# Tail tokens of two batches interleaved over all 128 partitions, with row patches on two queues and a new order of the closing steps

## The chip, the cores and the metric

The kernel runs on one core of one Trainium2 chip. The metric is the device time of one launch in microseconds, as the median of several runs; less is better. One execution has also been recorded by the hardware profiler, and all times of single instructions come from that execution. They count from the start of its span.

## The reference

The inputs are q, k and v (8 batches, 8 heads, 576 tokens, 64 per head) and the weights of a spectral layer: `w_r` and `w_i` (64 modes, 512 x 512 each) and `w_ch` (512 x 512). First comes causal attention with a window of 128 tokens and a linear bias per head. Its output x (8 x 576 x 512) goes through the spectral mix:

```
X = rfft(x, axis=1)                      # along the tokens
Y[:, :64] = X[:, :64] times (w_r + i w_i), one 512x512 matrix per mode
y = irfft(Y, n=576, axis=1)
u = x + y
out = u + max(u @ w_ch, 0)               # float32, 8 x 576 x 512
```

The output has 9.44 MB.

## The kernel before

**Stages.** Up to about 150 us the attention runs, unit by unit of a batch and four heads. From then to about 409 us the 64 modes are streamed: `acc` gathers the products of the transformed tokens with `w_r` and `w_i`, four modes at a time (a "quad"). The loads of the weights set the pace there. While they stream, TensorE also prepares what can be had early: the tokens times `w_ch` (`XW`) and, for all modes but the last ones, the rows of `Z` (mode rows of y) and of `ZW` (mode rows of y @ w_ch). From about 409 us the last quad is worked up, and then come the closing steps, in which the output is made and stored. Everything that the change touches takes effect in these closing steps.

**Tiles of the output.** 576 tokens are four tiles of 128 tokens and a tail of 64. A unit j of `units` is a pair of batches and one tile, so 128 x 2 x 512 outputs, 512 KB. Units 0 to 3 are batches 0 and 1, units 4 to 7 batches 2 and 3, 9 to 12 batches 4 and 5, and 13 to 16 batches 6 and 7. Units 8 and 17 hold the tails: unit 8 those of batches 0 to 3, unit 17 those of batches 4 to 7. In a tail unit before the change, batch b lies in the lower 64 partitions and batch b + 1 in the upper 64, and the second half of the free axis holds batches b + 2 and b + 3.

**Steps.** Two steps make a unit, and the order of all steps is a string written out by hand. `activate(j)`, written `a` and the unit's number, is the channel side: `begin` puts `XW` into the PSUM pair `mm`, `channels` adds the inverse transform of the upper modes' `ZW` (through `spread`, L626, with a quarter of the array per matmul), and ScalarE writes `r = relu(mm)`. For a unit in `POOLED`, GpSimd then adds the tokens x to r. `finish(j)`, written `f` and the number, is the token side: for a unit that is not in `POOLED`, `add_tokens` puts x into the PSUM pair `yy` through an identity matmul; `finish_tokens` adds the inverse transform of `Z`; VectorE writes `o = yy + r` (L780), and the store of `o` is issued. For a unit in `HALVES` the ScalarE and VectorE work and the store go in two pieces. `mm` and `yy` have two buffers each, `r` has six, `o` five.

**Queues.** SP issues the stores of full tiles (L782), each 512 KB, or 256 KB for half a unit. A tail unit is stored by two transfers of 64 partitions each (L790): one from SP for the lower half, one from GpSimd's queue for the upper half.

**Row patches.** The last quad's rows of `Z` and `ZW` [...] `patch` (L616) copies them by small transfers, one per batch. The steps wait for them: `a` of a pair of batches for its rows of `ZW`, `f` for its rows of `Z`. After the last matmul of the stream, SP patches `Z` of batches 0 and 1 and `ZW` of batch 0. GpSimd's queue patches, in this order, `Z` of batches 2, 3, 4, then `ZW` of 1, 2, 3, then `Z` of 5, 6, 7, then `ZW` of 4, 5, 6, 7. Its additions for `POOLED` units stand behind these on the same engine.

Of the kernel before, what the change touches and what calls it, by code (L numbers as in the profile page):

```python
# [11 lines left out]
BF16 = mybir.dt.bfloat16  # L12
# [8 lines left out]
P = 128  # L21
# [6 lines left out]
FULL = 4  # L28
# [371 lines left out]
def kernel(  # L400
# [10 lines left out]
    nc = tc.nc  # L411
# [11 lines left out]
    ident = const.tile([P, P], BF16, name="ident")  # L423
    F = const.tile([P, FULL + 2, 2 * NM], BF16, name="F")
    FT = const.tile([P, 2, S], BF16, name="FT")
# [33 lines left out]
    with ExitStack() as actx:  # L459
        at = _Attention(tc, actx, q, k, v, (ident, F, FT), x, XC, raw)  # L460
        n = len(at.units)
# [49 lines left out]
        for stage in range(min(lags), n + max(lags)):  # L511
            for name, arg, lag in STAGE:
                run(name, arg, stage - lag)
                if name in ("transpose", "exp") and side.get(stage):
                    for _ in range(1 + (name == "transpose")):
                        fn, h = side[stage].pop(0)
# [3 lines left out]
            if stage in AHEAD:  # L520
                if stage:
                    b, g = at.units[stage - 1]
# [5 lines left out]
    with ExitStack() as mctx:  # L528
# [14 lines left out]
        def late_end(acc, g, n):  # L543
# [19 lines left out]
            late_channels(zw, yT, yw, slice(0, DM))  # L563
            patch([(nc.gpsimd, b) for b in range(B)], yw, g, lambda b: ZW[:, b // 2, 1])

# [25 lines left out]
        ROWS = (LO, HI)  # L591

        def spectra(hf, bp, z, zw):
# [6 lines left out]
            for et in range(4):  # L600
                nc.tensor.matmul(zw, lhsT=lhsT[et], rhs=wch[:, et],
                                 start=(et == 0), stop=(et == 3))
            nc.scalar.copy(ZW[:, bp, hf], zw)  # L603
            for i in range(2):
# [7 lines left out]
        def patch(todo, rows, g, dst, lo=0, hi=8):  # L612

            for queue, b in todo:
                r = 64 * (b % 2) + 8 * (g % 8)
                queue.dma_start(out=dst(b)[r + lo : r + hi],  # L616
                                in_=rows.rearrange("(k v) e -> k v e", v=16)[lo:hi, b])

        def tokens(st, half):
            o = st * P + (64 * half if st < FULL else 0)  # L620
            return slice(o, o + 64)

        def spread(dst, half, b, hf, st, tok):

            row = ROWS[(b % 2) ^ (1 - hf)]
            nc.tensor.matmul(  # L626
                dst[ROWS[half]], lhsT=FT[row, b % 2, tokens(st, tok)], rhs=ZW[row, b // 2, hf],
                start=False, stop=True, skip_group_check=True,
            )

        units = []
# [5 lines left out]
        def token_tiles(j):  # L637
            b, st = units[j]
            return x[:, b : b + 2, st] if st < FULL else x[:, b + 1 : b + 4 : 2, FULL]
# [39 lines left out]
            if j + 1 < len(units):  # L679
                transposed(j + 1)  # L680

        POOLED, HALVES, FIRST = (3, 4, 8, 12, 16), (0, 1, 2, 7, 15), (0, 1)
        mms, yys, rs = {}, {}, {}

        def pair(tag, slot=0):
# [7 lines left out]
        def begin(j):  # L693

            slot = idle.pop(0)
            mm = pair("mm", slot)
            mms[j] = mm, slot
            b, st = units[j]
            for row in range(2):
                for n in range(2):  # L700
                    dst, c = (row, n) if st < FULL else (n, row)
                    nc.tensor.matmul(
                        mm[ROWS[c], dst], lhsT=ident[ROWS[row], ROWS[row]],
                        rhs=XW[ROWS[row], j, n], start=True, stop=False, skip_group_check=True,
                    )

        def channels(j):

            mm, b, st = mms[j][0], *units[j]
            for row in range(2):  # L710
                for n in range(2):
                    if st < FULL:
                        spread(mm[:, row], n, b + row, 1, st, n)
                    else:
                        spread(mm[:, n], row, b + row + 2 * n, 1, st, 0)

        def last_rows(ps, j, rows):

# [23 lines left out]
        def add_tokens(j):  # L742

            yy = yys[j][0]
            for n in range(2):
                nc.tensor.matmul(yy[:, n], lhsT=ident, rhs=token_tiles(j)[:, n],
                                 start=True, stop=False, skip_group_check=True)

        def finish_tokens(j):

            yy, b, st = yys[j][0], *units[j]
            for n in range(2):
                if st < FULL:
                    nc.tensor.matmul(  # L754
                        yy[:, n], lhsT=FT[:, n, st * P : (st + 1) * P], rhs=Z[:, b + n],
                        start=j in POOLED, stop=True, skip_group_check=True,
                    )
                    continue
                for half in range(2):
                    nc.tensor.matmul(  # L760
                        yy[ROWS[half], n], lhsT=FT[:, half, FULL * P :],
                        rhs=Z[:, b + half + 2 * n],
                        start=j in POOLED, stop=True, skip_group_check=True,
                    )

        def finish(j):

            b, st = units[j]
            if j == 0:
                last_rows(yys[0][0], 0, heads["yq"])  # L770
            else:
                if j not in yys:
                    take(j)
                if j not in POOLED:
                    add_tokens(j)
                finish_tokens(j)
            (yy, slot), r = yys.pop(j), rs.pop(j)
            o = heads["out"].tile([P, 2, DM], FP32, tag="o", bufs=5, name="o")
            for c in parts(j):
                nc.vector.tensor_tensor(out=o[:, c], in0=yy[:, c], in1=r[:, c], op=ALU.add)  # L780
                if st < FULL:
                    nc.sync.dma_start(  # L782
                        out=out[b + c.start : b + c.stop, st * P : (st + 1) * P].rearrange(
                            "b p e -> p b e"),
                        in_=o[:, c],
                    )
                    continue
                for half in range(2):
                    lo, hi = b + half + 2 * c.start, b + half + 2 * c.stop - 1
                    (nc.gpsimd if half else nc.sync).dma_start(  # L790
                        out=out[lo:hi:2, FULL * P :].rearrange("b p e -> p b e"),
                        in_=o[ROWS[half], c],
                    )
            free.append(slot)

        quads, side, recycle = [], [], list(again)
        ZW = Z = XW = FM = wch = w2 = None
        K1 = again[-1] + 1
        LAST = NM // 4 - 1
        for g in range(NM // 4):  # L800
# [5 lines left out]
            for i in range(8):  # L806
# [21 lines left out]
                for a in range(4):  # L828
                    nc.tensor.matmul(  # L829
                        into[32 * (i // 2) : 32 * (i // 2) + 32],  # L830
                        lhsT=window[a],
                        rhs=w[a],
                        start=(ri == 0 and a == 0), stop=(ri == (m > 0) and a == 3),
# [7 lines left out]
                if k == K1 - 1:  # L841
                    actx1.close()
                    w2 = mctx.enter_context(
                        tc.tile_pool(name="w2", bufs=NWB, side="right", reuse_waits="tile")
                    )
                    load_w(NWB, w2, False)
                    right = mctx.enter_context(
                        tc.tile_pool(name="late", bufs=1, side="right", reuse_waits="tile")
                    )
                    wch = right.tile([P, 4, DM], BF16, name="wch")  # L850
                    nc.gpsimd.dma_start(out=wch, in_=moe_w_ch.rearrange("(a p) e -> p a e", p=P))
                    ZW = right.tile([P, B // 2, 2, DM], BF16, name="ZW")
                    Z = right.tile([P, B, DM], BF16, name="Z")
                    XW = right.tile([P, len(units), 2, DM], BF16, name="XW")
                    FM = right.tile([P, 2, 2 * P], BF16, name="FM")
                    nc.gpsimd.memset(FM, 0.0)
                    for b in range(2):
                        nc.gpsimd.dma_start(
                            out=FM.rearrange("(k v) b s -> k v b s", v=16)[:, b, b],
                            in_=FT[64 * b + 56 : 64 * b + 64, b, : 2 * P],  # L860
                        )

                if quads:
                    if next(quads[0], True):
# [20 lines left out]
        yq, yT = heads[LAST]  # L885
# [10 lines left out]
                                    ident[96:, 96:])  # L896
            nc.vector.tensor_copy(yT[:, 2 * i : 2 * i + 2, 96:], tr[:, 2 * i : 2 * i + 2, 96:])
        patch([(nc.sync, 0), (nc.sync, 1)], yq, LAST, lambda b: Z[:, b])
        patch([(nc.gpsimd, b) for b in (2, 3, 4)], yq, LAST, lambda b: Z[:, b], 6)
        yw = F[:, : DM // (2 * NM)].rearrange("p a b -> p (a b)")  # L900
        for i, c in enumerate(sides):
            late_channels(zl[i], yT, yw, c)
# [8 lines left out]
        free.append(1)  # L911
        take(1)
        begin(1)
        channels(1)
        channel_rows = partial(patch, rows=yw, g=LAST, dst=lambda b: ZW[:, b // 2, 1])
        channel_rows([(nc.sync, 0)] + [(nc.gpsimd, b) for b in (1, 2, 3)])
        patch([(nc.gpsimd, b) for b in (5, 6, 7)], yq, LAST, lambda b: Z[:, b], 6)
        channel_rows([(nc.gpsimd, b) for b in (4, 5, 6, 7)])

        for step in ("a0 f0 a1 f1 a3 a2 f2 a7 f7 a4 f3 a5 f5 a16 a9 f4 f9 a12 a17 f16 f17 a8 "  # L920
                     "a13 f12 f13 a11 f11 a14 f8 a10 f14 a6 f10 f6 a15 f15").split():
            {"a": activate, "f": finish}[step[0]](int(step[1:]))


# [28 lines left out]
```

The softmax here doesn't subtract the row's maximum and nothing guards it: scores larger than these inputs give would overflow.

## Time and profile before

| what | us |
|---|---|
| median of 4 runs | 452.65 |
| lowest and highest | 451.78, 453.04 |
| the profiled execution, its own time | 452.27 |
| its span | 449.9 |
| TensorE busy | 355.3 |
| VectorE busy | 177.1 |
| ScalarE busy | 152.5 |
| GpSimd busy | 70.5 |

The span runs from the first to the last recorded instruction; the profiled execution's time has 2.4 us more around it. Engines: PE is TensorE's matmuls and PEld its weight loads, DVE is VectorE, ACT ScalarE, POOL GpSimd, SP SyncE; SPq is SP's queue. A busy share is an average over stages with different limits, so the closing steps have to be read in windows of their own. PEclk is the granted TensorE clock; it is 1.00 from 408 us until TensorE has done its work.

### The profile page before, as it was taken

How to read it: one execution, taken by the hardware profiler on the slowest of the kernel's cores; microseconds unless marked ns; L12 is line 12 of the kernel's file. 1: busy time of each engine (PE TensorE's matmuls, PEld its weight loads, DVE VectorE, ACT ScalarE, POOL GpSimd, SP SyncE). 2: the span in 40 equal slices, each digit the busy share in tenths (PEclk: the TensorE clock that was granted, in tenths of full speed). 3: DMA queues.
4: the chain of work that ended last, by engine and by line, in shares of the span. 5: the costliest groups of instructions: out<-in, count | busy, mean ns of one | idle time of the engine just before them, and what ended most of it. 6: DMA issues, size and time to landing. Idle time of an engine off the chain costs nothing.

```text
span 449.9 us, 8002 instructions
## 1 busy us (share of the span) xinstructions
PE 355.3 (79%) x3301; PEld 190.5 (42%) x3326; DVE 177.1 (39%) x322; ACT 152.5 (34%) x195; POOL 70.5 (16%) x125
## 2 busy tenths in 40 slices
PE   4788899999866485657467767999999999877992
PEld 3457777777653132212222233544444444323330
DVE  7879899998832011000010222121212202301783
ACT  6869899999810000000000010211122110101861
POOL 8600101012411100100000000000000000074960
PEclk8589999999999566675975798999999999999997
DMA  8999999999999999999999999999999999994697
GB/s 281 316 311 321 309 298 310 317 299 248 200 290 316 307 278 318 327 377 425 420 422 422 420 422 420 422 421 417 422 419 421 421 418 421 421 389 149 239 339 270
DMA packets 53524, 157.03 MB, mean 349 GB/s; under 512 B 5217, under 2 KB 24433, under 8 KB 41073
## 3 DMA queue, kind: packets, MB, share of 16 engines
q1 hardware_dynamic: 47440, 140.02, 80.9%
q0 software_dynamic: 6048, 16.50, 18.5%
q8 instruction: 26, 0.43, 0.4%
q14 instruction: 10, 0.07, 0.0%
HBM read 162.53 MB, written 9.44 MB: 382 GB/s over the span
## 4 chain that ended last, share of the span: by engine, by line
DMA 54%; PE 28%; DVE 10%; issue 2%; POOL 1%; SPq 1%; ACT 1%; DVEq 0%; POOLq 0%; ACTq 0%
DMA w<-in_moe_w_i_dram 17%; DMA w<-in_moe_w_r_dram 15%; DMA vr<-in_v_dram 12%; PE acc L829 10%; DMA vr<-in_moe_w_i_dram 8%; PE my L669 7%; DVE vb L233 3%; PE tr L648 2%; PE my L626 2%; DMA kr<-in_k_dram 2%; DVE x L347 1%; DVE att L305 1%; DVE k L238 1%; PE yy L754 1%; DVE vt L235 1%
## 5 line engine op out<-in xcount | busy, mean ns | idle before, releaser
L829 PE MATMUL acc<-w,XC 128*32 128x512 bf16 x456 | 129.7, 450 | 43.4 <-DMA w<-in_moe_w_r_dram 22.4
L829 PEld LDWEIGHTS <-XC 128*32 128x32 bf16 x508 | 59.3, 140 | 127.0 <-issue 92.7
L294 ACT ACTIVATE att<-sc 128x1024 bf16<-128x1024 f32 x64 | 64.0, 1031 | 8.3 <-PE sc L284 8.3
L603 ACT CAST ZW<-zw 128x512 bf16<-128x512 f32 x8 | 4.7, 586 | 159.8 <-DVE Z L605 126.5
L575 DVE TENSOR_SCALAR yq<-acc 128x512 bf16<-128x512 f32 x13 | 8.9, 688 | 105.2 <-PE acc L829 105.2
L678 ACT CAST XW<-my 128x512 bf16<-128x512 f32 x36 | 19.3, 589 | 77.6 <-PE my L626 77.6
L616 POOL DMA_DIRECT2D Z<-yq x20 | 10.3, 519 | 216.8 <-issue 210.3
L331 PE MATMUL av<-vb,att 128*128 128x132 bf16 (+1 forms) x576 | 38.4, 217 | 5.9 <-DVE x L347 4.2
L331 PEld LDWEIGHTS <-att 128*128 128x128 bf16 x704 | 36.5, 98 | 11.5 <-DVE x L347 8.5
L650 DVE COPY xT<-tr 128x1024 bf16<-128x1024 bf16 x18 | 12.4, 691 | 71.9 <-PE tr L648 71.9
L669 PE MATMUL my<-wch,xT 128*64 128x512 bf16 x288 | 34.5, 382 | 0.8 <-DVE xT L650 0.8
L256 ACT COPY qkT<-tp 128x1152 bf16<-128x1152 bf16 x30 | 33.5, 1115 | 2.4 <-PE tp L250 1.8
L284 PE MATMUL sc<-qkT 64*64 64x256 bf16 (+2 forms) x640 | 25.7, 269 | 5.2 <-ACT qkT L256 1.6
L347 DVE TENSOR_TENSOR x<-av,rec 128x640 bf16<-128x640 f32 x32 | 26.4, 824 | 1.1
L780 DVE TENSOR_TENSOR o<-yy,r 128x1024 f32<-128x1024 f32 (+1 forms) x23 | 21.8, 988 | 6.7 <-ACT r L737 3.4
L284 PEld LDWEIGHTS <-qkT 64*64 64x64 bf16 x640 | 14.8, 110 | 19.5 <-issue 16.2
L669 PEld LDWEIGHTS <-xT 128*64 128x64 bf16 x288 | 14.8, 109 | 19.0 <-issue 6.9
L233 DVE CAST vb<-vr 64x1024 bf16<-64x1024 f32 x32 | 22.2, 694 | 0.2
L737 ACT ACTIVATE r<-mm 128x1024 f32<-128x1024 f32 (+1 forms) x23 | 18.2, 838 | 7.5 <-PE mm L626 6.6
L305 DVE TENSOR_TENSOR att<-att,mask 128x1024 bf16<-128x1024 bf16 x32 | 20.6, 683 | 0.0
L605 DVE CAST Z<-z 64x512 bf16<-64x512 f32 x16 | 11.0, 689 | 22.9 <-PE z L598 22.7
L523 POOL COPY gate<-x 1x1 bf16<-1x1 bf16 x11 | 5.8, 524 | 86.1 <-DVE x L347 86.1
(124 smaller groups left out, 376.3 us busy)
## 6 DMA issues: line engine op xcount, KB each, us to landing
w<-in_moe_w_i_dram SPq DMA_DIRECT2D x52, 1024.0 KB, 17.0
w<-in_moe_w_r_dram SPq DMA_DIRECT2D x45, 1024.0 KB, 16.8
qr<-in_q_dram SPq DMA_DIRECT2D x16, 576.0 KB, 7.6
kr<-in_k_dram SPq DMA_DIRECT2D x16, 576.0 KB, 8.0
vr<-in_v_dram SPq DMA_DIRECT2D x64, 128.0 KB, 6.1
w<-in_moe_w_r_dram POOLq DMA_DIRECT2D x16, 512.0 KB, 17.4
out_dram<-o SPq DMA_DIRECT2D x11, 512.0 KB, 3.2
w<-in_moe_w_i_dram POOLq DMA_DIRECT2D x6, 512.0 KB, 7.5
```

Source lines behind the costliest of these rows:

```text
L233: nc.vector.tensor_copy(self.vb[u % 2][row, :, :, :, W * half : W * half + D], src[row, :2])
L256: (self.nc.vector.tensor_copy if u < 2 and w == "q" else self.nc.scalar.copy)(dst.rearrange("q h (p j) -> q h p j", j=TPP), tp.rearrange(" ...
L284: nc.tensor.matmul(sc[64 * half : 64 * half + 64, e, j * 256 + c0 : j * 256 + c0 + n], lhsT=qkT[row, 1, h, k0 + j : k0 + P : 2], rhs=qkT[r ...
L294: self.nc.scalar.activation(self.att[u % 2][:, kt * 8 * P : (kt + 1) * 8 * P], sc.rearrange("p e n -> p (e n)"), AF.Exp, scale=1.0 / math. ...
L305: nc.vector.tensor_tensor(out=rows, in0=rows, in1=self.table[:, heads], op=ALU.mult)
L331: nc.tensor.matmul(bank[:, qt * W : qt * W + rhs[j].shape[1]], lhsT=att[:, o : o + P], rhs=rhs[j], start=(n == 0 and j == 0), stop=(n == l ...
L347: nc.vector.tensor_tensor(out=self.x[:, b, :, cs].rearrange("p t (h d) -> p h t d", h=2), in0=tiles[:, :, :, :D], in1=rec.unsqueeze(-1).br ...
L669: nc.tensor.matmul(mm[ROWS[half]], lhsT=lhsT, rhs=wch[:, dt], start=(dt == 0), stop=False, skip_group_check=True,)
L678: nc.scalar.copy(XW[:, j, n], mms[n])
L737: nc.scalar.activation(r[:, c], mm[:, c], AF.Relu)
L780: nc.vector.tensor_tensor(out=o[:, c], in0=yy[:, c], in1=r[:, c], op=ALU.add)
L829: nc.tensor.matmul(into[32 * (i // 2) : 32 * (i // 2) + 32], lhsT=window[a], rhs=w[a], start=(ri == 0 and a == 0), stop=(ri == (m > 0) and ...
```

## The change

The change has four parts. They all lie in the work on units and patches.

1. Tail tokens alternate. In units 8 and 17, partition 2p holds token p of one batch and partition 2p + 1 token p of the other. Three tables made once, by a fill and six copies on GpSimd during the weight stream, do the interleaving inside the matmuls: `pairs` (a permutation, in the place of the identity), `FI` (the inverse transform of the tail with alternating columns, zero elsewhere) and `FC` (the same for the channel side). `begin` and `channels` of a tail unit are then two full matmuls each instead of four small ones, `finish_tokens` four full ones instead of four of 64 columns.
2. A tail unit is stored by two transfers of 128 partitions and 256 KB from SP, each one for two batches. GpSimd stores nothing any more.
3. `Z` of batch 2 is patched from SP. GpSimd's queue patches `Z` of 3, 4, 5, 6, then `ZW` of 1, 2, 3, then `Z` of 7, then `ZW` of 4 to 7.
4. `POOLED`, `HALVES` and the order of the steps are new. The tail units are no longer in `POOLED`, and they come last.

```diff
-        POOLED, HALVES, FIRST = (3, 4, 8, 12, 16), (0, 1, 2, 7, 15), (0, 1)
+        POOLED, HALVES, FIRST = (3, 6, 9, 12, 13, 14, 15), (0, 1, 2, 5, 8), (0, 1)
...
-            for row in range(2):
-                for n in range(2):
-                    dst, c = (row, n) if st < FULL else (n, row)
+            for n in range(2):
+                if units[j][1] == FULL:
+                    nc.tensor.matmul(mm[:, n], lhsT=pairs, rhs=XW[:, j, n],
+                                     start=True, stop=False, skip_group_check=True)
+                    continue
+                for row in range(2):
                     nc.tensor.matmul(
-                        mm[ROWS[c], dst], lhsT=ident[ROWS[row], ROWS[row]],
-                        rhs=XW[ROWS[row], j, n], start=True, stop=False, skip_group_check=True,
+                        mm[ROWS[row], n], lhsT=ident[ROWS[n], ROWS[n]],
+                        rhs=XW[ROWS[n], j, row], start=True, stop=False, skip_group_check=True,
                     )
...
-            for row in range(2):
-                for n in range(2):
-                    if st < FULL:
-                        spread(mm[:, row], n, b + row, 1, st, n)
-                    else:
-                        spread(mm[:, n], row, b + row + 2 * n, 1, st, 0)
+            for n in range(2):
+                if st == FULL:
+                    nc.tensor.matmul(mm[:, n], lhsT=FC, rhs=ZW[:, b // 2 + n, 1],
+                                     start=False, stop=True, skip_group_check=True)
+                    continue
+                for row in range(2):
+                    spread(mm[:, n], row, b + n, 1, st, row)
...
-                nc.tensor.matmul(yy[:, n], lhsT=ident, rhs=token_tiles(j)[:, n],
+                nc.tensor.matmul(yy[:, n], lhsT=ident if units[j][1] < FULL else pairs,
+                                 rhs=token_tiles(j)[:, n],
                                  start=True, stop=False, skip_group_check=True)
...
-                        yy[ROWS[half], n], lhsT=FT[:, half, FULL * P :],
-                        rhs=Z[:, b + half + 2 * n],
-                        start=j in POOLED, stop=True, skip_group_check=True,
+                        yy[:, n], lhsT=FI[:, half], rhs=Z[:, b + half + 2 * n],
+                        start=False, stop=True, skip_group_check=True,
...
-                for half in range(2):
-                    lo, hi = b + half + 2 * c.start, b + half + 2 * c.stop - 1
-                    (nc.gpsimd if half else nc.sync).dma_start(
-                        out=out[lo:hi:2, FULL * P :].rearrange("b p e -> p b e"),
-                        in_=o[ROWS[half], c],
+                for n in range(c.start, c.stop):
+                    nc.sync.dma_start(
+                        out=out[b + 2 * n : b + 2 * n + 2, FULL * P :].rearrange("h p e -> p h e"),
+                        in_=o[:, n],
                     )
...
+                    FI = right.tile([P, 2, P], BF16, name="FI")
+                    FC = right.tile([P, P], BF16, name="FC")
+                    pairs = right.tile([P, P], BF16, name="pairs")
+                    nc.gpsimd.memset(FI, 0.0)
+                    for i, rows in enumerate((slice(0, 64), slice(64, P))):
+                        nc.gpsimd.tensor_copy(FI[:, i, i::2], FT[:, i, FULL * P :])
+                        nc.gpsimd.tensor_copy(pairs[:, i::2], ident[:, rows])
+                        nc.gpsimd.tensor_copy(FC[rows], FI[rows, i])
...
-        patch([(nc.gpsimd, b) for b in (2, 3, 4)], yq, LAST, lambda b: Z[:, b], 6)
+        patch([(nc.sync, 2)] + [(nc.gpsimd, b) for b in (3, 4, 5, 6)], yq, LAST, lambda b: Z[:, b], 6)
...
-        patch([(nc.gpsimd, b) for b in (5, 6, 7)], yq, LAST, lambda b: Z[:, b], 6)
+        patch([(nc.gpsimd, 7)], yq, LAST, lambda b: Z[:, b], 6)
         channel_rows([(nc.gpsimd, b) for b in (4, 5, 6, 7)])

-        for step in ("a0 f0 a1 f1 a3 a2 f2 a7 f7 a4 f3 a5 f5 a16 a9 f4 f9 a12 a17 f16 f17 a8 "
-                     "a13 f12 f13 a11 f11 a14 f8 a10 f14 a6 f10 f6 a15 f15").split():
+        for step in ("a0 f0 a1 f1 a3 a2 f2 a5 f5 a6 a10 f3 f10 a15 a4 f6 f4 a13 a16 f15 f16 "
+                     "a12 f13 a11 a9 f11 f12 a7 a14 f7 a8 f9 a17 f14 f17 f8").split():
```

Up to the first closing step both programs issue the same work on TensorE, in the same order.

More of the change, by code (lines that the diff above doesn't have):

```diff
@@ L697, in begin @@
             mms[j] = mm, slot
-            b, st = units[j]
-            for row in range(2):
-                for n in range(2):
-                    dst, c = (row, n) if st < FULL else (n, row)
+            for n in range(2):
[4 more added lines that the diff above has]
+                for row in range(2):
                     nc.tensor.matmul(
-                        mm[ROWS[c], dst], lhsT=ident[ROWS[row], ROWS[row]],
-                        rhs=XW[ROWS[row], j, n], start=True, stop=False, skip_group_check=True,
+                        mm[ROWS[row], n], lhsT=ident[ROWS[n], ROWS[n]],
+                        rhs=XW[ROWS[n], j, row], start=True, stop=False, skip_group_check=True,
                     )
@@ L796 @@
         quads, side, recycle = [], [], list(again)
-        ZW = Z = XW = FM = wch = w2 = None
+        ZW = Z = XW = FM = FI = FC = pairs = wch = w2 = None
         K1 = again[-1] + 1
```

## The prediction

> **What bounds the kernel now.** The first view is the page's slices: up to some 409 us the weight stream holds the DMA near 420 GB/s, and nothing of the change reaches into that stage except a few table copies. So I read the closing steps, 418 us to the end, in windows of one microsecond (columns: length, then busy us and count of PE, PEld, DVE, ACT, POOL, then PEclk, the DMA's busy share, GB/s).
>
> ```profile
> 425.00:426.00 1.00, 1.00 (x13) 0.39 (x11) 1.00 (x2) 0.47 (x1) 0.94 (x1) 1.00 0.09 35
> 433.00:434.00 1.00, 0.98 (x10) 0.36 (x11) 1.00 (x2) 0.55 (x2) 1.00 (x1) 1.00 0.86 178
> 434.00:435.00 1.00, 1.00 (x11) 0.24 (x9) 0.92 (x2) 0.72 (x1) 0.85 (x1) 1.00 1.02 240
> 440.00:441.00 1.00, 1.00 (x8) 0.31 (x4) 0.81 (x2) 0.74 (x2) 0.00 (x0) 1.00 0.97 258
> 443.00:444.00 1.00, 0.00 (x0) 0.00 (x0) 0.00 (x0) 0.00 (x0) 0.00 (x0) 1.00 1.03 389
> ```
>
> Two things are full here: PE has no free time until 441.2, and the stores then run on for six more microseconds with every engine idle. So at the end the bound is the store queue, fed by a PE that is itself full. The queue has lost time in two ways: it starved at 425 (35 GB/s), and twice it was busy at a low rate (178 and 240 GB/s at 433 to 435, 258 at 440). The low rates are the tail units' stores, of 64 partitions each. The two store lines say so; the answer for L782 comes first, that for L790 second:
>
> ```profile
> L782 SPq DMA_DIRECT2D out_dram<-o x21: 332/372/1213, 417.7 to 444.1; - x21
> DMA to landing us min/median/max: 2.2/4.3/6.3
> ...
> L790 SPq DMA_DIRECT2D out_dram<-o x2: 725/792/860, 431.8 to 437.1; - x2
> DMA to landing us min/median/max: 4.7/5.0/6.5
> ```
>
> In the trace's packet records, a 2 KB packet of a full store takes 84 ns (16 engines, so 512 KB in 256/16 x 84 = 1.345 us); from 433.0 to 434.5, when the lower half of unit 17 is stored, the medians of half-microseconds are 149, 162 and 193 ns. Last, PE's own steps and their waits:
>
> ```profile
> 424.14 0.41 PE L702 MATMUL mm<-XW,ident 64*64 64x512 bf16 x4
> 424.70 0.80 PE L626 MATMUL mm<-ZW,FT 64*64 64x512 bf16 x4
> ...
> 427.72 0.60 PE L702 MATMUL mm<-XW,ident 64*64 64x512 bf16 x4
> 428.15 0.60 PE L626 MATMUL mm<-ZW,FT 64*64 64x512 bf16 x4
> 428.68 0.60 PE L754 MATMUL yy<-Z,FT 128*128 128x512 bf16 x2
> 429.12 0.59 PE L746 MATMUL yy<-x,ident 128*128 128x512 bf16 x2
> 429.65 0.62 PE L760 MATMUL yy<-Z,FT 128*64 128x512 bf16 x4
> 430.20 0.65 PE L702 MATMUL mm<-XW,ident 64*64 64x512 bf16 x6
> ...
> 435.11 0.62 PE L760 MATMUL yy<-Z,FT 128*64 128x512 bf16 x4
> 435.66 0.41 PE L702 MATMUL mm<-XW,ident 64*64 64x512 bf16 x4
> 435.90 0.39 PE L626 MATMUL mm<-ZW,FT 64*64 64x512 bf16 x4
> 436.22 0.61 PE L746 MATMUL yy<-x,ident 128*128 128x512 bf16 x2
> ...
> 437.19 0.41 PE L702 MATMUL mm<-XW,ident 64*64 64x512 bf16 x4
> ```
>
> From start to start: an ordinary `a` takes 435.66 to 436.22, 0.56 us; an `f` with its tokens 436.22 to 437.19, 0.97; a pooled `f` 428.68 to 429.12, 0.44, and 0.53 where a change of shape follows (f3, 422.08 to 422.61 in the same view). The tail steps are a17 0.96 (427.72 to 428.68), f17 1.08 (429.12 to 430.20), f8 0.55 (435.11 to 435.66). The first two lines are a16: 0.5 us lost waiting for the `ZW` rows of batches 6 and 7.
>
> **The change part by part: PE.** Three more ordinary units are pooled (seven, was four): -3 x 0.43 = -1.3 us. Full matmuls follow each other at 0.216 us (two tokens matmuls 0.43). A tail `a` becomes four of them, 0.87 and a change of shape of 0.1: 0.97. A tail `f` becomes six, 1.40: f17 +0.3, f8 +0.85, since it also loses its pooling.
>
> What a tail `a` cost before is where a rule speaks against the change. The trace has 0.96. The Trainium skill (TensorE: Matmul & The Clock Gate, Part 3: Packing small matmuls) says that small matmuls on different tiles of the array run together, so eight quarter matmuls should take the 0.56 of an ordinary `a`, and full ones would add 0.4 for each tail. The row decides: a17 ran only two at a time (its four L702 rows start at 427.72 and 427.93), as both of `n` use the same two quarters. So 0 for a17, 0.1 for a8 (with a13 it took 1.42, less 0.56). By the row the PE sum is -1.3 + 0.3 + 0.85 + 0.1 = 0; by the rule +0.7. I take 0.
>
> **Patches.** SP gets one more small issue (0.6 us) between its `Z` patches and its `ZW` of batch 0. It ends at about 415.7, and `ZW` waits for its rows until 415.63 anyway; the first store is at 417.70. On POOL:
>
> ```profile
> 416.37 1.64 POOL L616 DMA_DIRECT2D ZW<-F  x3 [0.95 <-ACT F L570]
> 418.00 1.55 POOL L616 DMA_DIRECT2D Z<-yq  x3
> 419.54 2.16 POOL L616 DMA_DIRECT2D ZW<-F  x4
> ```
>
> The fourth `Z` patch of the first group fits into the 0.95 us that POOL waits for F, and two of the three at 418.00 are gone, so `ZW` of 4 to 7 is issued at 418.5 to 420.7, 1.0 us earlier, and POOL's additions begin at 420.7 instead of 421.7.
>
> Against this, a10 needs `ZW` of 4 and 5 and moves from near the end to the eleventh place. The steps a5, f5, a6 before it cost what a7, f7, a4 cost in their place, and a4 ended at 422.08; so a10 begins then and wants its rows at 422.32. The landings of that stretch have a straggler: one DMA engine was held 1.2 us by a 16 KB instruction fetch at 420.3. The patches issued at 418.53 and 419.04 had 15 of 16 parts by 420.85 and 421.86, and the last at 423.04 and 423.68. `ZW` of 5 will be issued at 419.07, so I put it at 423.7. The bounds: 422.0 (no straggler, no stall) and 425.0 (the longest landing of L616, 5.9 us). So PE stands 1.3 us (0 to 2.6) before a10; f3, f10 and everything after stand behind it, and the next store with them. The 0.5 us before a16 goes, as a15 comes three us after its rows.
>
> **Sum on PE.** a10 ends at 424.0. Then come 7 pooled `f` x 0.53, 5 `f` x 0.97, 9 `a` x 0.56, 2 tail `a` x 0.97 and 2 tail `f` x 1.40: 18.4 us. With 0.15 where a9 waits for ScalarE to free its buffer, PE ends at 442.5 (441.2 before).
>
> **Stores.** o3 leaves DVE (1.22 us) at 425.8; its packets start 0.86 after (as of the store issued at 425.14). So the starved gap is 425.0 to 426.7, 0.7 longer. From there 14 units at 1.345 are 18.8 us: 445.5, with small gaps (0.5) 446.0, and 0.4 to the landing. From the other side: f8's halves leave DVE at 443.25 and 443.85, and the last 256 KB needs at least the 2.2 of L782, with the SP issue as slow as L790's (0.79) 2.9: 446.1 to 446.8. Both say 446.5. Before, the last landing was at 448.8 and the span ended 1.1 after. The new span is 447.6; I add 0.4 for the DMA engine that is behind, as landings of one store lay up to 1.9 apart at the end: **448.0, against 449.9, so -1.9 us**. In the profiled execution that is 452.27 to 450.4; its own time lies 0.38 under the median, so the median goes from 452.65 to about **450.7**.
>
> That rests on the new tail stores running at 84 ns a packet. The trace has no such store. Its nearest row by shape, L790, says 149 to 193 ns; the Trainium skill (SBUF — State Buffer, Door 1: The DMA port swizzle) says that 64 partitions reach half of the 16 ports and all 128 reach all. By the row four tail stores at the end cost 4 x 1.3 us, by the rule 4 x 0.67: 2.6 us apart. I take the rule, for the full stores next to it have 128 partitions and 84 ns.
>
> **At nothing.** The tables: seven GpSimd instructions behind 183.7, where POOL has nothing until 394; if POOL were not idle they would delay the patches of the last-but-one quad. POOL's two more additions (2.13 each): it loses two store issues (0.65 each) and starts 1.0 earlier; a14's r is ready at about 439.5 and VectorE turns to f14 at 439.9, a margin of 0.3 to 0.4. VectorE keeps 1.22 beside them: o<-yy,r takes 1.224 at 423.9 with POOL adding and 1.225 at 437.3 without. SP's two extra-long tail issues are in the 2.9 above.
>
> **The rivals.** (1) a10 does not wait: the straggler comes elsewhere and the rows land by 422.3. Then everything is 1.3 earlier: span 446.5, median 449.3. For it: 15 of 16 parts were there by 421.9. Against: the fetch follows from PE's place in its program, which is the same up to here. Chance 0.13. (2) The gain goes under: the stall is 2.6, or the store queue starves again wherever PE feeds it two `a` in a row. Span 449.0 to 449.9, median 452.2; 0.15. For it: PE, not the queue, would then set the end, and it ends later. (3) Slower: the tail stores are slow as such and now stand last, with nothing behind to overlap. From 442.6, four of them at x us each, then 1.5 to the end: 450.8 (slower by over 0.9) is reached from x = 1.7, or 210 ns a packet. At 291 ns, the longest in L790's time, x = 2.3, span 453.4, median 456. For it: L790 is also slow to issue (0.79 against 0.37). 0.12. That the change doesn't do what it says is no separate case: its stores could only fail as in (3).
>
> **Numbers.** The forecast has 0.60. A measurement of this kernel tells about 0.2%, 0.9 us, from no change. Faster is forecast and (1), 0.73; same is (2), 0.15; slower (3), 0.12. The range takes in (1) and (2): 449.0 to 452.6.
>
> **What would show it.** Right: no slow window with GB/s under 300 at a full share after 427; the last store lands within 3 us of its issue; a10's L626 starts near 423.7; PE ends near 442.5 and the stores near 446.5. Wrong: tail packets over 150 ns; a wait of a10 over 3 us; DMA gaps after 428.

## The result and the profile after

The changed kernel has a median of 452.33 us over 35 runs, the kernel before 453.33 over 56 runs beside them. The ratio is **0.9972, interval 0.9959 to 0.9985**: faster by 0.28%, which is 1.3 us of 453 (0.7 to 1.9). The forecast was 1.95 us. (The prediction started from 452.65, the median of the first 4 runs of the kernel before.) The profiled execution took 450.89 us with a span of 448.8, against 452.27 and 449.9: the span is 1.1 us shorter where 1.9 were forecast.

The span moves with the weight stream, which the change doesn't touch: in the profiles shown below the stream ends anywhere from 411.8 to 415.0 us. So the kernels are compared here by their **closing span**, from the start of the matmul `zl<-wch,ident`, the first after the stream, to the end of the span. It was 37.01 us before (412.88 to 449.90) and is 35.94 after (412.82 to 448.76). Each is read from one profile; the timed ratio stands beside it.

The windows of the changed kernel, in the columns used above:

```profile
425.00:426.00 1.00, 1.00 (x18) 0.38 (x16) 1.00 (x2) 0.06 (x2) 0.36 (x1) 1.00 0.08 29
426.00:427.00 1.00, 0.66 (x9) 0.21 (x3) 0.98 (x2) 1.00 (x2) 0.00 (x0) 1.00 0.26 96
434.00:435.00 1.00, 1.00 (x17) 0.38 (x16) 1.00 (x2) 0.32 (x2) 1.00 (x2) 1.00 1.03 377
440.00:441.00 1.00, 0.94 (x6) 0.36 (x4) 0.91 (x2) 0.00 (x0) 0.00 (x0) 1.00 1.04 391
445.00:446.00 1.00, 0.00 (x0) 0.00 (x0) 0.00 (x0) 0.00 (x0) 0.00 (x0) 0.50 1.01 381
446.00:447.00 1.00, 0.00 (x0) 0.00 (x0) 0.00 (x0) 0.00 (x0) 0.00 (x0) 0.50 0.18 68
447.00:448.00 1.00, 0.00 (x0) 0.00 (x0) 0.00 (x0) 0.00 (x0) 0.00 (x0) 0.50 0.03 10
```

The slow windows are gone: 377 and 391 GB/s where there were 240 and 258. The starved gap is longer: 425 to 426.7 instead of 425 to 426. The last two lines are the surprise. At 446 to 448 the DMA is nearly idle (0.18, then 0.03) and yet the kernel waits. The landing records say for what. A store counts as done when its sixteen parts have landed, and the last stores of the changed kernel landed like this:

```
last packets of the store   15 of 16 parts   the 16th
issued at 442.27            445.26           446.53
issued at 443.35            445.95           447.15
issued at 444.02            446.62           447.79
```

One part in sixteen is late in every store that lands after 437 us, by 1.8 us at first (438.40 against 440.18) and by 1.2 in the end, and in none of those that land from 428 to 436 (there all sixteen lie within 0.3). At 437.12 the trace has one packet of 16 KB on the instruction queue, which took 948 ns. It is the one packet of this line of the DMA view from 436 to 439 us (packets, MB, share of the 16 engines):

```profile
q8 instruction: 1, 0.02, 2.0%
```

TensorE's program is fetched in such pieces: the recorded weight loads and matmuls between two of them are 254 on average in this trace, 184 to 349 in single cases. The one before came at 420.1 and took 1532 ns.

The other place is a10, in the timeline of TensorE:

```profile
421.92 0.39 PE L704 MATMUL mm<-XW,ident 64*64 64x512 bf16 x4
422.91 0.40 PE L626 MATMUL mm<-ZW,FT 64*64 64x512 bf16 x2 [0.61 <-DMA ZW<-F]
423.55 0.40 PE L626 MATMUL mm<-ZW,FT 64*64 64x512 bf16 x2 [0.23 <-DMA ZW<-F]
423.88 0.61 PE L758 MATMUL yy<-Z,FT 128*128 128x512 bf16 x2
```

a10's first matmuls run at 421.92 and its last at 423.55, where without a wait they would run at 422.14. The first pair waits for the `ZW` rows of batch 4 (15 parts landed by 421.09, the last at 422.87), the second for those of batch 5 (15 by 421.97, the last at 423.50): 1.4 us in all for a sixteenth part, and f3 stands behind it.

### The profile page after: what moved, and what is told of

It is laid out like the page before. It is cut to its first block, busy times and chain, and to the rows that moved or that the text cites. A ratio compares the mean times of both kernels' runs of the same rounds, so it can differ in the third digit from the quotient of the medians.

```text
span 448.8 us, 7986 instructions
## 1 busy us (share of the span) xinstructions
PE 356.0 (79%) x3290; PEld 190.4 (42%) x3314; DVE 177.1 (39%) x322; ACT 152.2 (34%) x195; POOL 74.5 (17%) x131
## 4 chain that ended last, share of the span: by engine, by line
DMA 54%; PE 30%; DVE 9%; issue 2%; ACT 1%; POOL 1%; SPq 1%; POOLq 1%; DVEq 0%; ACTq 0%
DMA w<-in_moe_w_r_dram 29%; PE acc L831 11%; DMA vr<-in_v_dram 9%; PE my L669 7%; DMA vr<-in_moe_w_r_dram 7%; DMA w<-in_moe_w_i_dram 6%; DVE vb L233 3%; PE tr L648 2%; PE my L626 2%; DMA qr<-in_q_dram 2%; PE av L331 1%; DMA kr<-in_k_dram 1%; PE yy L758 1%; DMA ZW<-F 1%; DVE k L238 1%
## 5 line engine op out<-in xcount | busy, mean ns | idle before, releaser
L831 PE MATMUL acc<-w,XC 128*32 128x512 bf16 x456 | 132.0, 455 | 41.3 <-DMA w<-in_moe_w_r_dram 22.8
L331 PEld LDWEIGHTS <-att 128*128 128x128 bf16 x704 | 36.5, 98 | 11.1 <-DVE x L347 8.1
L669 PEld LDWEIGHTS <-xT 128*64 128x64 bf16 x288 | 14.8, 109 | 18.9 <-issue 6.9
```

Source lines behind the costliest of these rows:

```text
L331: nc.tensor.matmul(bank[:, qt * W : qt * W + rhs[j].shape[1]], lhsT=att[:, o : o + P], rhs=rhs[j], start=(n == 0 and j == 0), stop=(n == l ...
L669: nc.tensor.matmul(mm[ROWS[half]], lhsT=lhsT, rhs=wch[:, dt], start=(dt == 0), stop=False, skip_group_check=True,)
L831: nc.tensor.matmul(into[32 * (i // 2) : 32 * (i // 2) + 32], lhsT=window[a], rhs=w[a], start=(ri == 0 and a == 0), stop=(ri == (m > 0) and ...
```

## The experiments

Theory A: full-width tail stores bring the gain; the order gives part of it back at a10; and the instruction fetch at 437 puts one DMA engine behind, which the full store queue keeps behind up to the end. Its rivals differ by run: that the late part has nothing to do with the fetch, that the order or the patches bring the gain, that the width of a store matters little. "PE ends" is the end of the last matmul. All ratios are to the kernel before on the same chip.

| run | ratio (95% interval) | closing span, us | PE ends, us of it | last store: 15 parts, 16th |
|---|---|---|---|---|
| before | 1 | 37.01 | 28.3 | spread over 1.9 |
| changed | 0.9972 (0.9959 to 0.9985) | 35.94 | 28.9 | 33.8, 35.0 |
| x1_fetch_late | 0.9925 (0.9898 to 0.9952) | 33.48 | 27.5 | 32.5, 32.5 |
| x2_fetch_early | 0.9931 (0.9902 to 0.9961) | 34.41 | 27.6 | 32.4, 33.4 |
| x3_tails_only | 0.9971 (0.9944 to 0.9998) | 35.86 | 29.5 | 34.0, 34.9 |
| x4_old_patches | 0.9991 (0.9965 to 1.0017) | 36.27 | 29.2 | 34.1, 35.2 |
| x5_order | 0.9928 (0.9902 to 0.9954) | 34.24 | 27.7 | 32.3, 33.3 |
| x6_half_stores | 1.0056 (1.0030 to 1.0081) | 39.50 | 29.0 | spread over 0.9 |
| x7_tails_only_fetch_late | 0.9935 (0.9910 to 0.9960) | 34.96 | 29.5 | 34.0, 34.0 |
| x8_before_fetch_late | 0.9991 (0.9970 to 1.0013) | 37.08 | 28.3 | spread over 1.9 |
| x9_order_fetch_late | 0.9918 (0.9886 to 0.9951) | 33.51 | 27.7 | 32.5, 32.5 |

**x1_fetch_late.** Only the number of warm-up matmuls at the very start changes, 400 us away from the place in question.

```diff
-        for _ in range(24):
+        for _ in range(2):
             nc.tensor.matmul(wt, lhsT=ident, rhs=ident, start=True, stop=True)
```

> The changed kernel with 2 instead of 24 warm-up matmuls at the very start, so that TensorE's program is 44 instructions shorter ahead of the closing steps and nothing in the closing steps changes. In the traces a 16 KB instruction fetch comes with every 256 TensorE instructions, at 420.1 and 437.1 us in the changed kernel, and the last parts of every store after 437 land 1.2 us after the other fifteen. Theory A (the fetch at 437 puts one DMA engine behind, the full store queue keeps it behind, and that is the 0.8 us that the prediction lacks): the last fetch falls behind the end of the program, all sixteen parts of the last store land within 0.3 us, and the fetch of 420 comes at about 422.5, behind the patches that a10 waits for, so that its wait of 1.3 us shrinks to under 0.5. The closing span (from the zl<-wch,ident matmul near 412.8 to the end; 37.0 us before, 35.9 after) becomes 33.7 to 34.6. Theory B (the late engine is late for its own sake, or from the tail stores' shape): one part still lands 1 us behind and the closing span stays at 35.9 +- 0.3, or loses 0.3 from a10 alone.

The fetches came at 9.1 us of the closing span and at 35.5, after the end (7.3 and 24.3 in the changed kernel). The sixteen parts of the last store landed within 0.3 us. a10 had its rows: TensorE's timeline, and then the last windows:

```profile
420.87 0.39 PE L704 MATMUL mm<-XW,ident 64*64 64x512 bf16 x4
421.09 0.47 PE L626 MATMUL mm<-ZW,FT 64*64 64x512 bf16 x4
421.49 0.60 PE L758 MATMUL yy<-Z,FT 128*128 128x512 bf16 x2
```

```profile
443.00:444.00 1.00, 0.00 (x0) 0.00 (x0) 0.00 (x0) 0.00 (x0) 0.00 (x0) 1.00 0.73 275
444.00:445.00 1.00, 0.00 (x0) 0.00 (x0) 0.00 (x0) 0.00 (x0) 0.00 (x0) 0.82 0.00 0
```

The second of these lines is not what the changed kernel showed: the DMA goes from 0.73 to nothing, with no thin trail. The closing span fell by 2.46 us, a little more than expected. The time is 0.75% under the kernel before: the same closing steps, instruction for instruction, give 1.3 us or about 3.4, by where the fetches fall. Theory A holds, and the rival falls. The fetch at 9.1 us still makes a part late (by 0.9 us at 423.33), but no step waits for it.

**x2_fetch_early.** The program is made longer instead of shorter, so that only the first fetch leaves the critical place.

```diff
-        for _ in range(24):
+        for _ in range(36):
...
-            for _ in range(3):
+            for _ in range(5):
                 wt = ps.tile([P, DM], FP32, tag="my", bufs=2, name="my")
```

> The changed kernel with 12 more warm-up matmuls at the start and 22 more during the last weights of the stream: TensorE's program is 68 instructions longer ahead of the closing steps, which are themselves unchanged. The fetches should come near 416.5, before the first store, and near 432. Theory A: a10's rows are no longer late by one part, its wait of 1.3 us falls to 0.3 or less and the starved gap at 425 to 426.5 shrinks by the same; but the second fetch again puts one engine about 1.2 us behind up to the end. Closing span 34.6 to 35.2 (35.9 in the changed kernel). Theory B (the fetch has nothing to do with either): a10 waits 1.3 us as before, closing span 35.9 +- 0.3. If the additional matmuls hold up the stream, its end (409.0) comes later, which the closing span leaves out.

The fetches came at 2.6 and 18.9 us. a10 waited for nothing, PE ended as in x1, and the last part was late again, by 1.0 us, with the thin trail at the end:

```profile
443.00:444.00 1.00, 0.00 (x0) 0.00 (x0) 0.00 (x0) 0.00 (x0) 0.00 (x0) 1.00 1.01 383
444.00:445.00 1.00, 0.00 (x0) 0.00 (x0) 0.00 (x0) 0.00 (x0) 0.00 (x0) 0.59 0.09 33
445.00:446.00 1.00, 0.00 (x0) 0.00 (x0) 0.00 (x0) 0.00 (x0) 0.00 (x0) 0.50 0.01 4
```

So the two costs come apart: 1.53 us from the rows of a10 (35.94 to 34.41), 0.93 from the late part at the end (34.41 to 33.48). The split rests on one profile of each run; the timed ratios of x1 and x2 don't tell these two apart. It is also the control for x1: a longer start gives most of the same gain, so the gain isn't from a shorter start.

**x3_tails_only.** The kernel before with the tables, the tail matmuls and the tail stores of the change, in the old order:

```diff
-        POOLED, HALVES, FIRST = (3, 4, 8, 12, 16), (0, 1, 2, 7, 15), (0, 1)
+        POOLED, HALVES, FIRST = (3, 4, 12, 16), (0, 1, 2, 7, 15), (0, 1)
...
-                for half in range(2):
-                    lo, hi = b + half + 2 * c.start, b + half + 2 * c.stop - 1
-                    (nc.gpsimd if half else nc.sync).dma_start(
-                        out=out[lo:hi:2, FULL * P :].rearrange("b p e -> p b e"),
-                        in_=o[ROWS[half], c],
+                for n in range(c.start, c.stop):
+                    nc.sync.dma_start(
+                        out=out[b + 2 * n : b + 2 * n + 2, FULL * P :].rearrange("h p e -> p h e"),
+                        in_=o[:, n],
                     )
```

> The kernel before with the interleaved tail units and their stores of 128 partitions alone: old order, old patches, old sets of pooled and halved units, except that unit 8 can't be pooled any more. Theory A (the full-width stores bring the gain, and the new order and patches give some back): no slow window at 433 to 435 and 440 to 442, tail packets at 84 to 88 ns instead of 149 to 193; PE ends 1.25 later, at about 442.4; closing span 35.0 to 36.0 against 37.0 before. Rival (the order and the patches bring the gain): closing span 36.6 to 38, as PE has 1.25 us more to do and sets the end.

It has the whole gain by itself: closing span 35.86, ratio 0.9971 against 0.9972. PE ends 1.2 later than before, as expected, and the stores make more than that good. The windows of its two tail units:

```profile
433.00:434.00 1.00, 0.95 (x10) 0.31 (x4) 1.00 (x2) 0.48 (x1) 0.00 (x0) 1.00 1.03 385
440.00:441.00 1.00, 1.00 (x11) 0.26 (x10) 1.00 (x2) 0.07 (x1) 0.00 (x0) 1.00 1.01 379
```

(From 434 to 435 it has 303 GB/s at a share of 0.84: there the queue ran short, and its packets still took 86 to 88 ns.) So with the fetches about where they were, the new order, the sets and the patches add nothing measurable to the tail units. x3 changes three things at once in those units: the width of their stores, the queue of half of them (GpSimd's before, SP's now) and their matmuls.

**x4_old_patches.** The changed kernel with the old patches:

```diff
-        patch([(nc.sync, 2)] + [(nc.gpsimd, b) for b in (3, 4, 5, 6)], yq, LAST, lambda b: Z[:, b], 6)
+        patch([(nc.gpsimd, b) for b in (2, 3, 4)], yq, LAST, lambda b: Z[:, b], 6)
...
-        patch([(nc.gpsimd, 7)], yq, LAST, lambda b: Z[:, b], 6)
+        patch([(nc.gpsimd, b) for b in (5, 6, 7)], yq, LAST, lambda b: Z[:, b], 6)
```

> The changed kernel with the patches on the queues and in the order of the kernel before. Theory A: ZW of batches 4 and 5 is issued 1.0 us later, a10 waits about 1 us longer (to 424.5), POOL's first addition begins 1.0 later, and the closing span grows from 35.9 to 36.5 to 37.0. Rival (the last part of these patches is late because of one DMA engine and not because of the place in the queue): the wait of a10 stays within 0.3 us and the closing span at 35.9 +- 0.3.

A miss for both. The closing span grew by 0.33, less than theory A asks and just over the rival's bound. a10 in its timeline:

```profile
420.86 0.39 PE L704 MATMUL mm<-XW,ident 64*64 64x512 bf16 x4
422.65 0.55 PE L626 MATMUL mm<-ZW,FT 64*64 64x512 bf16 x4 [1.41 <-DMA ZW<-F]
```

It is over at 423.20, 11.4 us into the closing span, where the changed kernel's a10 is over at 423.95, 11.1 us into its own. The rows of batch 5, the last that it waits for, are issued 1 us later, but their last part lands only 0.3 later (422.76, 11.0 us into the closing span, against 423.50, 10.7): most of the 1 us is lost in a wait that was there anyway, which is what the rival says. How much the place in GpSimd's queue still counts isn't shown, since the fetch itself came 0.5 us earlier in this run (6.8 us into the closing span against 7.3). The timed ratio (0.9991) is unclear against the changed kernel, as the intervals overlap.

**x5_order.** The changed kernel with a10 behind four steps that don't need its rows:

```diff
-        for step in ("a0 f0 a1 f1 a3 a2 f2 a5 f5 a6 a10 f3 f10 a15 a4 f6 f4 a13 a16 f15 f16 "
+        for step in ("a0 f0 a1 f1 a3 a2 f2 a5 f5 a6 f3 a4 f4 a15 a10 f6 f10 a13 a16 f15 f16 "
```

> The changed kernel with another order of eight steps: f3, a4, f4 and a15 come ahead of a10, so that a10 stands where its rows have landed; the instruction fetches stay where they are (near 7.4 and 24.3 us of the closing span). Theory A (two separate costs: the late rows of a10, and the engine that the second fetch puts behind): PE no longer waits for ZW, the starved gap of the stores shrinks by about 1.2, PE ends 1.2 earlier, and the last part of the last store is still 1.2 behind the others. Closing span 34.5 to 35.0 (35.94 in the changed kernel, 34.41 with the first fetch moved ahead). Rival (the late engine is all): closing span 35.6 to 36.2.

No wait for `ZW` is left, PE ends at 27.7, and the closing span is 34.24, somewhat better than expected. Its end has the thin trail, since a second fetch still falls into the last stores (at 22.6 us of the closing span, 24.3 in the changed kernel):

```profile
445.00:446.00 1.00, 0.00 (x0) 0.00 (x0) 0.00 (x0) 0.00 (x0) 0.00 (x0) 0.89 0.67 252
446.00:447.00 1.00, 0.00 (x0) 0.00 (x0) 0.00 (x0) 0.00 (x0) 0.00 (x0) 0.50 0.05 18
```

**x6_half_stores.** The changed kernel with the tail units and stores of the kernel before, that is the store part of x3's diff turned round, with the small matmuls.

> The changed kernel with the tail units of the kernel before: batches in halves, small matmuls, four stores of 64 partitions for each of the last units from SP and GpSimd, in the new order with the tail units last. Theory A (the stores of 64 partitions are slow by themselves, 178 to 258 GB/s instead of 380): 1 MB at about 220 GB/s and nothing behind to overlap, so about 2 us more, less 0.7 of shorter tail matmuls: closing span 37 to 38.5 (35.94 in the changed kernel). Rival (the slow windows of the kernel before came from two queues meeting in its middle, and the stores' width matters little): closing span 35.3 to 36.2.

Slower than before, and by more than expected: closing span 39.50, so 3.6 us more than the changed kernel. Its last windows:

```profile
446.00:447.00 1.00, 0.00 (x0) 0.00 (x0) 0.00 (x0) 0.00 (x0) 0.10 (x1) 0.79 1.01 197
447.00:448.00 1.00, 0.00 (x0) 0.00 (x0) 0.00 (x0) 0.00 (x0) 0.00 (x0) 0.50 0.97 307
448.00:449.00 1.00, 0.00 (x0) 0.00 (x0) 0.00 (x0) 0.00 (x0) 0.00 (x0) 0.50 0.89 262
449.00:450.00 1.00, 0.00 (x0) 0.00 (x0) 0.00 (x0) 0.00 (x0) 0.00 (x0) 0.50 0.64 223
```

197 to 307 GB/s, where the changed kernel has 381 in its last full window. So the tails can stand last only with their new stores. The expectation took off 0.7 us for shorter tail matmuls; PE in fact ended at 29.0, no earlier than in the changed kernel (28.9). It also counted four half stores for each unit, where unit 17 has two and unit 8 has four.

x6 brings back the width and GpSimd's queue together, so it doesn't decide between them. The packet records do for SP's stores. These are the medians of the packets that start in half a microsecond:

```
half us from        2 KB packets (SP)   4 KB packets (GpSimd's queue)
before, 433.0       152 ns              none
before, 433.5       162 ns              none
before, 440.0        84 ns              285 ns
before, 440.5        84 ns              316 ns
x6, 446.0           162 ns              none
x6, 448.0            84 ns              234 ns
```

Where SP's half stores run alone, their packets take about twice the 84 ns of a full store: with no packet from GpSimd's queue beside them, the width is left as the cause. In the other stretches SP's packets take 84 ns again, and the slow ones are GpSimd's (159 ns at their fastest). Whether those are slow by their 64 partitions or by their queue is not shown: no run has full stores on that queue or half stores on SP alone.

**x7_tails_only_fetch_late.** x3 with the fetch moved:

```diff
-        for _ in range(24):
+        for _ in range(2):
...
-            for _ in range(3):
+            for _ in range(2):
                 wt = ps.tile([P, DM], FP32, tag="my", bufs=2, name="my")
```

> The kernel before with the interleaved tail units alone (as in x3_tails_only, closing span 35.86), and TensorE's program 66 instructions shorter ahead of the closing steps (22 warm-up matmuls less at the start, 11 less during the last weights), so that the last fetch falls behind the end. Theory A: every part of the last stores lands within 0.3 us and the closing span falls by about 1.1 to 34.6 to 34.9; the rest up to the 33.48 of x1_fetch_late, some 1.2, is what the new order, the pooled set and the patches are worth once no fetch is in the way. Rival (order, pooled set and patches are worth nothing in any case, as x3 alone equals the changed kernel): closing span 33.4 to 33.9.

34.96: 0.9 less than x3, with all parts together at the end, and 1.48 more than x1. Its last windows have no trail:

```profile
446.00:447.00 1.00, 0.00 (x0) 0.00 (x0) 0.00 (x0) 0.00 (x0) 0.00 (x0) 0.59 0.75 281
447.00:448.00 1.00, 0.00 (x0) 0.00 (x0) 0.00 (x0) 0.00 (x0) 0.00 (x0) 0.50 0.00 0
```

Once no fetch is in the way, the new order, sets and patches are worth 1.5 us of closing span; in x1 PE ends about 2 us earlier. The timed ratios (0.9935 and 0.9925) don't tell these two apart.

**x8_before_fetch_late.** The same two edits on the kernel before.

> The kernel before, unchanged in the closing steps, with TensorE's program 66 instructions shorter ahead of them, so that the last fetch falls behind the end. Theory A (the fetch costs the kernel before less, since its half stores put engines out of step in any case): the closing span falls from 37.01 to 35.9 to 36.5, the landings of the last store still lie 0.7 us or more apart, and the change is worth 2.4 to 3.0 us against x1_fetch_late (33.48). Rival (the fetch costs both kernels the same, or more before): 35.5 or less, and the change is worth under 2.0 with the fetch away.

A miss for both: 37.08, nothing gained. The landings of its last store spread over 1.9 us as before, without a fetch after 10.3 us of the closing span. The slow windows and the trail are there all the same:

```profile
433.00:434.00 1.00, 1.00 (x12) 0.34 (x10) 0.92 (x2) 0.92 (x1) 1.00 (x1) 1.00 1.04 223
439.00:440.00 1.00, 1.00 (x12) 0.31 (x4) 1.00 (x2) 0.55 (x2) 0.00 (x0) 1.00 0.97 254
447.00:448.00 1.00, 0.00 (x0) 0.00 (x0) 0.00 (x0) 0.00 (x0) 0.00 (x0) 0.50 0.04 16
```

The spread is 0.6 us in the last full store ahead of the half stores of unit 17, 1.2 in the stores just behind these, and 1.9 to 2.5 from those of unit 8 on. So in the kernel before the half stores set it, and moving the second fetch takes nothing away. Which engines are late there isn't recorded. With the fetches away the change is worth 3.6 us of closing span (37.08 to 33.48), not 1.1: 2.1 from the tail units (37.08 to the 34.96 of x7) and 1.5 from the rest. By the timed ratios (0.9991 and 0.9925) the whole is 0.66%, or 3.0 us.

x8 is a second control for x1: a shorter program alone doesn't make a kernel measurably faster.

**x9_order_fetch_late.** x5's order and x1's shorter start.

> The changed kernel with both repairs: the order of x5_order, where a10 stands behind f3, a4, f4 and a15, and TensorE's program 44 instructions shorter ahead of the closing steps, as in x1_fetch_late. Theory A (the two costs lie in different places: the late rows of a10 at the first fetch, the late engine at the second): x5_order has 34.24 us of closing span and its last part 1.0 behind the others, so 33.1 to 33.5 here, no more than 0.4 under x1_fetch_late (33.48), where the first fetch had moved too and a10 no longer waited. Rival (the gains add up): 34.24 less the 2.46 of x1_fetch_late, 31.8.

33.51, the same as x1; the gains don't add up. When the first fetch moves, a10 has no wait that a better order could remove. Timed, x9 has the lowest ratio, 0.9918, but x1, x2 and x5 lie within its interval. All four beat both kernels, x2 by the least: its interval and the changed kernel's just overlap.

## Why the prediction was right or wrong

- **Direction and cause: right.** The new tail stores take away the slow windows (x3, x6). The rule taken for the packets held: tail packets took 84 to 88 ns, as the neighbours' do. Rival (3) described what slow stores at the end cost, and x6 shows it: it came about with half stores there, not with the new ones. One reading was too simple: only the first slow window (433 to 435) has SP's packets at 149 to 193 ns. In the second (440) SP's took 84 ns, and the slow packets were the 4 KB ones of GpSimd's queue; the 291 ns of rival (3) lies in their range.
- **a10: right.** Forecast 423.7, measured 423.55; the gap of the stores 425.0 to 426.7, as forecast. The reason was right too, one part held by the fetch (x1, x2).
- **PE: nearly.** Forecast 442.5, measured 441.73. (The prediction's own parts, 441.2 with 1.3 more before a10 and 0.5 less before a16, give 442.0.) The steps were priced with a change of shape behind each. An `a` behind an `a` took 0.46 (425.28 to 425.74) and not 0.56, and a pooled `f` before an `f` 0.44 (423.88 to 424.33) and not 0.53. It did not matter, since the store queue set the end.
- **Stores: right for fifteen parts, wrong for the sixteenth.** The last store was forecast to land at 446.5; fifteen parts did so by 446.62. **The failed step is the one that read "I add 0.4 for the DMA engine that is behind"; it measured 1.2** (447.79 against 446.62). That is the whole difference between the forecast span of 448.0 and the 448.8 of the profile. The prediction used the fetch of 420 to price a10 and did not ask for the next one, though the kernel before shows it, at 437.1. It took the 0.4 from the spread of landings in the kernel before; x8 shows that this spread came from the half stores, which the change removes, and x1 that the 1.2 us came from the fetch. Its own sign, a last store that lands within 3 us of its issue, failed for the same reason: 2.6 us for fifteen parts, 3.8 for the sixteenth.
- **The patches: the 1.0 us was not worth it.** `ZW` was issued earlier as forecast, but x4 lost only 0.33 of closing span without it.
- **"At nothing": held.** GpSimd's additions took 2.12 to 2.14 us as before, VectorE 1.22 beside them.

The timed gain, 1.3 us with an interval of 0.7 to 1.9, lies between the profile's 1.1 and the forecast.

## What to carry to other kernels

Where several DMA engines share the last transfers, look at when each part lands and not at the mean rate: a thin trail in the last windows, a share of 0.18 and 0.03 with everything else idle, can be one engine that was held up earlier. Ask of every instruction fetch that falls into a full DMA stretch what waits for the engine that serves it; a few instructions more or fewer far ahead in the program can move it out of the way. A change that makes two good moves can be measured as worth little because of such an accident, so do each of them alone, and with the accident moved, before throwing one away.

## What the runs showed of the hardware

A 16 KB piece of TensorE's program came with every 252 to 256 of its recorded instructions on average, by the run, and took 0.9 to 1.7 us near the closing steps, as one packet of the DMA. Where stores kept the queue full, one of their sixteen parts was late from then on, by 0.9 to 2.1 us at its worst. The rows for a10 were late in the same way (15 parts at 421.97, the last at 423.50). The full queue let that part catch up only slowly: from 1.8 to 1.2 us between the landings at 440.18 and 447.79 of the changed kernel, and in x5_order, behind its first fetch, from 1.8 to 0.3 between 423.64 and 433.93. Behind the starved gap of the changed kernel all sixteen were together again (at 428.68). So how much of a fetch is left at the end depends on how long before the end it came. Why the first lateness can be twice the 0.95 us of the packet is not shown. That it is the same engine throughout is inferred from the counts, since the trace doesn't name engines.

Stretches with stores of 64 partitions ran at 178 to 307 GB/s where those of 128 ran at about 380, and left the parts of the full stores behind them up to 2.2 us apart (x8).
